# Cosine attention with a gated MLP: norms of batch 0 by Ln and Exp, pair by pair, with copies and casts on other engines

## The chip, the cores and the metric

The kernel runs on one core of a Trainium2 chip. The metric is the device time of one execution in microseconds; lower is better. A core has five engines that work side by side, each in the order of its own instructions: TensorE (PE in the profile, with its weight loads apart as PEld), VectorE (DVE), ScalarE (ACT), GpSimd (POOL) and SyncE (SP), which here only issues DMA transfers. Times inside the kernel are counted from the start of the span.

## The reference

Eight batches, twelve heads, 448 tokens, head width 64. Attention works on q and k that are divided by their own norms; its output, with the heads side by side, goes through a two-layer MLP with the gate h * sigmoid(1.702 h).

```python
q_n = q / (np.linalg.norm(q, axis=-1, keepdims=True) + 1e-06)
k_n = k / (np.linalg.norm(k, axis=-1, keepdims=True) + 1e-06)
scores = np.matmul(q_n, k_n.transpose(0, 1, 3, 2)) / tau
scores = scores - np.max(scores, axis=-1, keepdims=True)
attn = np.exp(scores)
attn = attn / (np.sum(attn, axis=-1, keepdims=True) + 1e-09)
attn_out = np.matmul(attn, v)
# x: (B*S, H*D) = (3584, 768); w_in: (768, 2048); w_out: (2048, 768)
h = x @ w_in
g = h * (1.0 / (1.0 + np.exp(-1.702 * h)))
out = g @ w_out
```

tau is 0.1. All inputs and the output are float32.

## The kernel before

The unit of attention is a pair of heads: 48 pairs, six to a batch, numbered 0 to 47. A pair is loaded as three tiles, q, k and v, each of 112 partitions x 2 heads x 4 chunks x 64 (`load`, L227, 224 KB each). Then, for q and for k:

- ACT squares the tile (`square`, L235), DVE sums each row (`reduce`, L240).
- The sums of a group of pairs go together through the norms, which are wholly on DVE: an integer estimate of the inverse root, two Newton steps, and three operations for the 1e-6 (`norm_a` L252, `newton` L268, `norm_b` L278): ten DVE operations a group, whatever its size. For batch 0 the groups are pair 0; pairs 1 and 2; pairs 3, 4 and 5 (L608). Batch 1 has groups of two, the rest groups of three.
- POOL multiplies the tile with the inverse norm to float16 (`scale`, L291). Only q of pair 0 is scaled on DVE.
- For pairs 0 to 11, PE transposes the scaled tiles against an identity (`transposes`, L310) and DVE copies the result out (`transposed`, L325). Later pairs are transposed by DMA (`dma_transposed`, L329).

v is cast to float16 into a tile that holds ones for the softmax sums (`cast_v`, L302): by ACT for batch 0, by POOL later. There are six such v tiles.

Batches 0 and 1 run attention in halves of 224 query columns: `scores_h` on PE (L386), `exp` on ACT (L352), `attend_h` on PE (L402), `normalise_h` on DVE (L417), a transposition of the result back by PE (`turn_h`, L429), and a copy of this turned half into xT (`turned_h`, L438). In batch 0 the first half's copy is ACT's, the second half's DVE's. All first halves of batch 0 come ahead of the second ones, so that the MLP of batch 0 can begin on half the tokens. From batch 2 on attention runs on whole pairs, with the softmax sums exchanged through DRAM for three pairs at a time.

The MLP is a first product (`mm1_h` L525 for batch 0, `mm1` L496 for the others), a Tanh on ACT (L507), a gate on DVE (L513, L537), a second product (`mm2`, L550), and a copy with the factor 0.5 on ACT (`halve`, L562) before the store. A product of batch 0 needs the halves of all six pairs.

The order of the instructions is made before the program runs, by `Plan` (L36): every step is added with its engine, a cost in microseconds, a due time, what it follows, and which slots of buffers it takes and frees. The planner runs through these costs and takes, on each engine, the ready step that is due first. The order that comes out is then fixed on every engine, whatever the chip does. Some of its details matter here:

- Where PE has nothing to do for over 0.3 us of the plan within its first 50 us, it puts in transposes of the identity that nobody reads, to keep PE busy (`fill`, L322, and L57).
- Loads of q, k and v are issued by SP in one fixed order (`turn=True`); only q of pair 0 is issued by ACT. The w_in matrix (3 MB in two halves, L588) and w_out (the same, L594) are issued by POOL, in POOL's own order. w_in is held until q of pair 4 has landed, w_out until q of pair 11 has (L772 to L775).
- Pairs 6 to 8 may be loaded only when the first half of w_in has landed, pairs 9 to 11 when the second has, and pair 12, and what is behind it in SP's order, when w_out has (L620).
- The resource "port" (L607) keeps steps of POOL and norms of DVE from being planned side by side: what takes it on POOL is made to wait for the last step of DVE that took it (L66).

```python
groups = [(0,), (1, 2), (3, 4, 5)]
...
hold = [("w_in", int(x >= HP + 3))] if HP <= x < 2 * HP else [("w_out", 1)] if x == 2 * HP else []
```

Of the kernel before, what the change touches and what calls it, by code (L numbers as in the profile page):

```python
# [35 lines left out]
class Plan:  # L36
# [117 lines left out]
def kernel(  # L154
# [10 lines left out]
    nc = tc.nc  # L165
# [4 lines left out]
    P = 112  # L170
    C = S // P
    HP = H // 2
# [3 lines left out]
    NQK = 7  # L176
    HALF = 2 * HP
    AHEAD = 3
    TURN = 2 * HP
    SH = S // 2  # L180
    inv_tau = float(1.0 / tau)
# [6 lines left out]
    pool = lambda name, bufs: ctx.enter_context(tc.tile_pool(name=name, bufs=bufs))  # L188
# [5 lines left out]
    p_in = pool("p_in", NQK)  # L194
    p_v = pool("p_v", 4)
    p_sq = pool("p_sq", 2)
    p_n = pool("p_n", 2)
    p_qks = pool("p_qks", 3)
    p_qkT = pool("p_qkT", 7)
    p_exp = pool("p_exp", 8)  # L200
# [24 lines left out]
    q32, k32, v32, sqs, n2s, nrms, rss, qkss, qkTs = [{} for _ in range(9)]  # L225

    def load(x, d, src, nm):  # L227
# [4 lines left out]
            in_=src[b, h0 : h0 + 2].rearrange("h (p c) d -> p h (c d)", p=P),  # L232
        )

    def square(x, ti):  # L235
        sqs[x, ti] = p_sq.tile([P, 2, C, D], FP32, name="sq")
        src = (q32, k32)[ti][x]
        return nc.scalar.activation(out=sqs[x, ti], in_=src, func=AF.Square)  # L238

    def reduce(x, ti):  # L240
# [37 lines left out]
    def norm_b(grp):  # L278
# [9 lines left out]
            rss[x] = yv[:, x - grp[0]]  # L288
        return last

    def scale(x, ti, eng):  # L291
        if x not in qkss:
            qkss[x] = p_qks.tile([P, 2, C, 2, D], FP16, name="qks")
        src = (q32, k32)[ti].pop(x)
        return eng.tensor_tensor(  # L295
            out=qkss[x][:, ti].rearrange("p c j d -> p j c d"),
            in0=src,
            in1=rss[x][:, ti, :, :, None].to_broadcast((P, 2, C, D)),
            op=ALU.mult,
        )  # L300

    def cast_v(x):  # L302
        src = v32.pop(x)
        vt = vts[x % NV]
        copy = nc.scalar.copy if x < HP else nc.gpsimd.tensor_copy
        return tuple(
            copy(out=vt[:, :, j, 64 * j : 64 * j + D], in_=src[:, j]) for j in range(2)  # L307
        )
# [129 lines left out]
    def turned_h(x, h):  # L438
        b, hp = x // HP, x % HP
        if h == 0:  # L440
            xTs[b, hp] = p_x.tile([128, S], FP16, name=f"xT{hp}")
        (nc.scalar.copy if b + h == 0 else nc.vector.tensor_copy)(
            out=xTs[b, hp][:, h * SH : (h + 1) * SH],
            in_=avps.pop((x, h))[:, 384:].bitcast(FP16)[:, :SH],
        )
# [159 lines left out]
    )  # L605
    add = plan.add
    port = dict(takes=[("port", 1)], frees=[("port", 1)])  # L607
    groups = [(0,), (1, 2), (3, 4, 5)]  # L608
    groups += [tuple(range(g, g + 2)) for g in range(HP, HALF, 2)]
    groups += [tuple(range(g, g + GRP)) for g in range(HALF, NPAIR, GRP)]  # L610
    group_of = {x: g for g in groups for x in g}
# [5 lines left out]
    for x in range(NPAIR):  # L617
        s, grp, g, first = due_of(x), group_of[x], x // GRP, x < HP
        early = due_of(grp[0]) - (4 if first else 8)
        hold = [("w_in", int(x >= HP + 3))] if HP <= x < 2 * HP else [("w_out", 1)] if x == 2 * HP else []  # L620
        for ti, nm in ((1, "k"), (0, "q")):
            add(("load", nm, x), "ACT" if x + ti == 0 else "SP", 0.5, s - 13, partial(load, x, (q32, k32)[ti], (q, k)[ti], nm + "32"),
                takes=[(nm, 1)], dma=PAIR, hold=hold, turn=True)
            add(("sq", ti, x), "ACT", 0.53, early + ti * 0.1, partial(square, x, ti),
                after=[("load", nm, x)], takes=[("sq", 1)])
            add(("red", ti, x), "DVE", 0.6, early + 0.2, partial(reduce, x, ti),
                after=[("sq", ti, x)], frees=[("sq", 1)])
            dve = x == 0 and ti == 0
            add(("scale", ti, x), "DVE" if dve else "POOL", 0.7 if dve else 1.0, early + 0.5 if first else s - 5 - ti * 0.1,
                partial(scale, x, ti, nc.vector if dve else nc.gpsimd),  # L630
                after=[("norm", 1, grp)], takes=[("qks", 1), ("port", 1)], frees=[(nm, 1), ("port", 1)])
        if x == grp[0]:
            reds = [("red", ti, y) for y in grp for ti in range(2)]
            n = len(grp)
            add(("norm", 0, grp), "DVE", 0.78 + 0.06 * n, early + 0.3, partial(norm_a, grp), after=reds, **port)
            add(("norm", 1, grp), "DVE", 1.14 + 0.18 * n, early + 0.3, partial(norm_b, grp), after=[("norm", 0, grp)], **port)
        add(("load", "v", x), "SP", 0.5, s - 9, partial(load, x, v32, v, "v32"),
            takes=[("v", 1)], dma=PAIR, hold=hold, turn=True)
        add(("cast", x), "ACT" if first else "POOL", 0.64 if first else 0.75, s - 0.5, partial(cast_v, x),
            after=[("load", "v", x)], takes=[("vt", 1), ("port", 1 - first)], frees=[("v", 1), ("port", 1 - first)])  # L640
        if x < TURN:
            add(("tp", x), "PE", 0.4, s - 3, partial(transposes, x),
                after=[("scale", 0, x), ("scale", 1, x)], takes=[("a", 1), ("qkT", 1)], frees=[("qks", 2)])
            add(("qkT", x), "DVE", 0.6, s - 3, partial(transposed, x), after=[("tp", x)], frees=[("a", 1)])
        else:
            add(("qkT", x), "SP", 1.3, s - 3, partial(dma_transposed, x),
                after=[("scale", 0, x), ("scale", 1, x)], takes=[("qkT", 1)], frees=[("qks", 2)],
                dma=packets(2 * P, C * D * 4))
        if x < HALF:
            for h in range(2):  # L650
# [12 lines left out]
                add(("turn", x, h), "PE", 0.15, sh + 1, partial(turn_h, x, h), after=[("nx", x, h)],  # L663
                    frees=[("xs", 1)])
                add(("x", x, h), "ACT" if first and not h else "DVE", 0.35, sh + 1, partial(turned_h, x, h), after=[("turn", x, h)],
                    takes=[("x", 1 - h)], frees=[("mm", 1)])
            continue
        for c in range(C):
            add(("s", x, c), "PE", 0.19, s + c // 2, partial(scores, x, c), after=[("qkT", x)],
                takes=[("sp", 1)], frees=[("qkT", int(c == C - 1))], rows=64)  # L670
# [100 lines left out]
    for i in range(2):  # L771
# [2 lines left out]
        add(("w_out", i), "POOL", 1.0, 9 + i, partial(load_w_out, i), hold=[("load", "q", 2 * HP - 1)],  # L774
            dma=packets(1024, 3072), **port)  # L775

    make_identity(nc, ident)
    for vt in vts:
        nc.vector.memset(vt[:, :, 0, D:128], 0.0)
# [46 lines left out]
```

## Time and profile before

| What | Value |
|---|---|
| Median of 8 runs | 479.57 us (475.34 to 480.99) |
| Profiled execution, its own time | 480.99 us |
| Its span | 479.1 us |
| Busy: PE, ACT, DVE, POOL | 97%, 65%, 58%, 28% of the span |
| TensorE clock granted, mean | 0.989 of full speed |
| DMA moved | 63.50 MB, 133 GB/s over the span |
| Exp of the scores (L355, ACT) | 192 x 917 ns |
| Squares (L238, ACT) | 96 x 635 ns |
| Row sums (L244, DVE) | 96 x 678 ns |
| Scaling (L295, POOL) | 95 x 1046 ns |
| Cast of v on POOL (L307) | 84 x 401 ns |
| Identity transposes (L323, PE) | 326 x 234 ns |

Successive instructions overlap in the records: matmuls and transposes are issued much closer together than their single durations, and an ACT or DVE operation starts up to some 0.1 us before the record of the one before it ends. Where a step's place in a queue counts, the distance from start to start is what matters. A share of busy time says little about PE, since the identity transposes count as busy too. In brackets behind an instruction the timelines give the idle time before it and what ended it.

### The profile page before, as it was taken

How to read it: one execution, taken by the hardware profiler on the slowest of the kernel's cores; microseconds unless marked ns; L12 is line 12 of the kernel's file. 1: busy time of each engine (PE TensorE's matmuls, PEld its weight loads, DVE VectorE, ACT ScalarE, POOL GpSimd, SP SyncE). 2: the span in 40 equal slices, each digit the busy share in tenths (PEclk: the TensorE clock that was granted, in tenths of full speed). 3: DMA queues.
4: the chain of work that ended last, by engine and by line, in shares of the span. 5: the costliest groups of instructions: out<-in, count | busy, mean ns of one | idle time of the engine just before them, and what ended most of it. 6: DMA issues, size and time to landing. Idle time of an engine off the chain costs nothing.

```text
span 479.1 us, 9003 instructions
## 1 busy us (share of the span) xinstructions
PE 463.0 (97%) x3382; PEld 267.8 (56%) x3382; DVE 276.0 (58%) x663; ACT 310.3 (65%) x491; POOL 132.2 (28%) x189
## 2 busy tenths in 40 slices
PE   8789999899999999999999999999999999999996
PEld 8767889664444554445444554445444554555563
DVE  6736986787688635875495636963373315532500
ACT  4669978789897567876778567865666556423411
POOL 1450761657624322406151422415110000000000
PEclk9999999799999999999999999999999999999999
DMA  9999597989978557446564567343310222012022
GB/s 200 227 228 251 92 207 212 256 231 206 230 148 138 142 133 187 117 103 192 145 152 109 140 158 186 96 123 97 88 44 3 62 68 63 2 62 67 1 57 76
DMA packets 81435, 63.50 MB, mean 133 GB/s; under 512 B 40232, under 2 KB 74864, under 8 KB 81392
## 3 DMA queue, kind: packets, MB, share of 16 engines
q1 hardware_dynamic: 77504, 56.41, 47.9%
q0 software_dynamic: 3648, 6.29, 7.3%
q8 instruction: 26, 0.43, 0.4%
q10 hardware_dynamic: 240, 0.23, 0.1%
q14 instruction: 17, 0.14, 0.1%
HBM read 49.81 MB, written 11.14 MB: 127 GB/s over the span
## 4 chain that ended last, share of the span: by engine, by line
PE 75%; DMA 9%; DVE 5%; ACT 4%; POOL 2%; issue 2%; SPq 2%; ACTq 0%; POOLq 0%; DVEq 0%
PE mm L554 27%; PE mm L499 23%; PE avp L363 9%; PE sp L344 6%; DMA q<-in_q_dram 3%; DMA k<-in_k_dram 3%; PE mm L529 3%; PE mm L409 3%; ACT expT L355 2%; POOL qks L295 2%; DMA v<-in_v_dram 2%; PE sp L392 2%; DVE xT L487 1%; ACT sq L238 1%; PE tps L323 1%
## 5 line engine op out<-in xcount | busy, mean ns | idle before, releaser
L355 ACT ACTIVATE expT<-sp 112x896 f16<-112x896 f32 x192 | 166.7, 917 | 57.1 <-PE sp L344 45.8
L554 PE MATMUL mm<-w_out,gT 128*128 128x384 f16 x896 | 153.8, 326 | 0.0
L499 PE MATMUL mm<-xT,w_in 128*128 128x448 f16 x672 | 134.0, 353 | 1.1 <-DVE gT L516 0.9
L554 PEld LDWEIGHTS <-gT 128*128 128x128 f16 x896 | 84.1, 98 | 65.4 <-issue 13.0
L499 PEld LDWEIGHTS <-w_in 128*128 128x128 f16 x672 | 63.1, 98 | 67.7 <-issue 12.8
L516 DVE SCALAR_TENSOR_TENSOR gT<-th,mm 128x448 f16<-128x448 f16 x112 | 67.9, 618 | 57.0 <-ACT th L509 56.5
L509 ACT ACTIVATE th<-mm 128x448 f16<-128x448 f32 x128 | 69.4, 545 | 37.8 <-PE mm L499 31.4
L244 DVE TENSOR_REDUCE n<-sq 112x8 f32<-112x512 f32 x96 | 64.2, 678 | 38.5 <-ACT sq L238 38.0
L307 POOL CAST vt<-v 112x256 f16<-112x256 f32 x84 | 32.3, 401 | 160.8 <-PE avp L363 102.0
L380 DVE TENSOR_SCALAR av<-avp 65x448 f16<-65x448 f32 x72 | 44.5, 618 | 47.7 <-PE avp L363 47.4
L363 PE MATMUL avp<-expT,vt 112*128 112x448 f16 x288 | 66.6, 352 | 0.7 <-DVE av L380 0.6
L295 POOL TENSOR_TENSOR qks<-k,y 112x512 f16<-112x512 f32 x48 | 50.2, 1045 | 57.7 <-DVE y L285 33.2
L565 ACT ACTIVATE ost<-mm 128x384 f32<-128x384 f32 x56 | 27.5, 491 | 43.7 <-PE mm L554 42.1
L295 POOL TENSOR_TENSOR qks<-q,y 112x512 f16<-112x512 f32 x47 | 49.2, 1047 | 6.6 <-DVE xT L487 6.6
L344 PE MATMUL sp<-qkT 64*112 64x448 f16 x288 | 43.0, 372 | 0.0
L363 PEld LDWEIGHTS <-vt 112*128 112x128 f16 x288 | 27.8, 97 | 25.6 <-issue 1.3
L238 ACT ACTIVATE sq<-k 112x512 f32<-112x512 f32 x48 | 30.4, 636 | 13.4 <-DMA k<-in_k_dram 10.4
L487 DVE TENSOR_TENSOR xT<-av,rcb 64x448 f16<-64x448 f16 x72 | 31.4, 437 | 10.6 <-DMA rcb<-rcp 9.6
L238 ACT ACTIVATE sq<-q 112x512 f32<-112x512 f32 x48 | 30.2, 635 | 9.5 <-DMA q<-in_q_dram 6.7
L323 PE MATMUL tps<-ident 128*128 128x128 f16 x326 | 23.5, 234 | 5.8 <-DVE qkT L327 4.3
L344 PEld LDWEIGHTS <-qkT 64*112 64x112 f16 x288 | 13.1, 124 | 27.8 <-issue 27.5
L409 PE MATMUL mm<-vt,expT 112*112 112x65 f16 x384 | 25.7, 222 | 0.5 <-ACT expT L355 0.4
(39 smaller groups left out, 231.1 us busy)
## 6 DMA issues: line engine op xcount, KB each, us to landing
k<-in_k_dram SPq DMA_DIRECT2D x48, 224.0 KB, 2.9
v<-in_v_dram SPq DMA_DIRECT2D x48, 224.0 KB, 3.3
q<-in_q_dram SPq DMA_DIRECT2D x47, 224.0 KB, 4.9
rcb<-rcp SPq DMA_DIRECT2D x24, 168.0 KB, 3.2
w_in<-in_moe_w_in_dram POOLq DMA_DIRECT2D x2, 1536.0 KB, 17.5
w_out<-in_moe_w_out_dram POOLq DMA_DIRECT2D x2, 1536.0 KB, 14.8
out_dram<-ost SPq DMA_DIRECT2D x7, 336.0 KB
out_dram<-ost SPq DMA_DIRECT2D x8, 288.0 KB
```

The costliest lines, as they stand in the source:

```text
L238: return nc.scalar.activation(out=sqs[x, ti], in_=src, func=AF.Square)
L244: nc.vector.tensor_reduce(out=n2s[grp][:, x - grp[0], ti], in_=sqs.pop((x, ti)), axis=AX.X, op=ALU.add,)
L295: return eng.tensor_tensor(out=qkss[x][:, ti].rearrange("p c j d -> p j c d"), in0=src, in1=rss[x][:, ti, :, :, None].to_broadcast((P, 2, ...
L344: nc.tensor.matmul(out=sp[:, j, :S], lhsT=qkT[64 * j : 64 * (j + 1), 1, c * P : (c + 1) * P], rhs=qkT[64 * j : 64 * (j + 1), 0, :], start= ...
L355: nc.scalar.activation(out=e, in_=sps.pop(key)[:, :, :S], func=AF.Exp, scale=inv_tau, **kw)
L363: nc.tensor.matmul(out=ps, lhsT=vts[x % NV][:, c, j], rhs=exps[x, c][:, j], start=(c == 0), stop=(c == C - 1),)
L380: nc.vector.tensor_scalar(out=avs[x][:n, j], in0=ps[:n], scalar1=AV_SCALE, scalar2=None, op0=ALU.mult)
L409: nc.tensor.matmul(out=ps[:P, o : o + D + 1], lhsT=exps[x, h, c // 2][:, j, at : at + P], rhs=vts[x % NV][:, c, j, 63 * j : 63 * j + D + 1 ...
L499: nc.tensor.matmul(out=ps[:, :S], lhsT=w_in_sb[:, kk, 128 * m : 128 * (m + 1)], rhs=xTs[b, kk], start=(kk == 0), stop=(kk == KT1 - 1),)
L509: nc.scalar.activation(out=ths[key], in_=mms[key][:, :S], func=AF.Tanh, scale=0.851)
L516: nc.vector.scalar_tensor_tensor(out=gts[b // 2][:, m, (b % 2) * S : (b % 2 + 1) * S], in0=ths.pop((b, m)), scalar=1.0, in1=mms.pop((b, m) ...
L554: nc.tensor.matmul(out=mms[b2, t, n][:, :NW], lhsT=gts[b2][:, kk, 128 * t : 128 * (t + 1)], rhs=w_out_sb[:, kk, NW * n : NW * (n + 1)], st ...
```

## The change

It has three parts, all in the head of the kernel.

1. The norms of the six pairs of batch 0 are made pair by pair. ACT takes Ln of the sums and then Exp of half of it, which is the norm (`root`); DVE adds 1e-6 and takes the reciprocal (`inverse`). These take the place of the ten DVE operations, and they do not take the "port". A table set that holds Ln and Exp is loaded by ACT as its first instruction. The pool of the small norm tiles has three buffers instead of two. Later batches keep their norms.
2. The first halves' copies into xT in batch 0 are DVE's, like the others (`XA` is empty).
3. ACT casts v of pairs 0 and 1 only (`CA`), POOL that of all others.

The switch that could put squares on POOL (`SQP`) is empty, so it does nothing. As all this goes through the planner, the order changes on every engine. In the changed order, 259 identity transposes stand on PE where there were 326; POOL issues the first half of w_in after the scaling of pair 1, where it was after that of k of pair 0; and ACT has two loads of tables, one at its start and one before the first Tanh, where it had one.

```diff
+    SQP, SQT, XA, CA = (), (0, 1), (), (0, 1)
...
-    p_n = pool("p_n", 2)
+    p_n = pool("p_n", 3)
...
+    def root(grp):
+        a = n2s[grp]
+        nc.scalar.activation(out=a, in_=a, func=AF.Ln)
+        nc.scalar.activation(out=a, in_=a, func=AF.Exp, scale=0.5)
+
+    def inverse(grp):
+        a = n2s.pop(grp)
+        y = p_n.tile([P, len(grp), 2, 2, C], FP32, name=f"yv_{len(grp)}")
+        nc.vector.tensor_scalar(out=y, in0=a, scalar1=1e-6, scalar2=None, op0=ALU.add)
+        last = nc.vector.reciprocal(out=y, in_=y)
+        for x in grp:
+            rss[x] = y[:, x - grp[0]]
+        return last
...
-        copy = nc.scalar.copy if x < HP else nc.gpsimd.tensor_copy
+        copy = nc.scalar.copy if x in CA else nc.gpsimd.tensor_copy
...
-        (nc.scalar.copy if b + h == 0 else nc.vector.tensor_copy)(
+        (nc.scalar.copy if x in XA and not h else nc.vector.tensor_copy)(
...
-    groups = [(0,), (1, 2), (3, 4, 5)]
+    groups = [(x,) for x in range(HP)]
...
+            if first:
+                add(("norm", 0, grp), "ACT", 0.48, early + 0.3, partial(root, grp), after=reds)
+                add(("norm", 1, grp), "DVE", 0.45, early + 0.3, partial(inverse, grp), after=[("norm", 0, grp)])
+        if x == grp[0] and not first:
             add(("norm", 0, grp), "DVE", 0.78 + 0.06 * n, early + 0.3, partial(norm_a, grp), after=reds, **port)
             add(("norm", 1, grp), "DVE", 1.14 + 0.18 * n, early + 0.3, partial(norm_b, grp), after=[("norm", 0, grp)], **port)
...
-        add(("cast", x), "ACT" if first else "POOL", 0.64 if first else 0.75, s - 0.5, partial(cast_v, x),
-            after=[("load", "v", x)], takes=[("vt", 1), ("port", 1 - first)], frees=[("v", 1), ("port", 1 - first)])
+        ca = x in CA
+        add(("cast", x), "ACT" if ca else "POOL", 0.64 if ca else 0.75, s - 0.5, partial(cast_v, x),
+            after=[("load", "v", x)], takes=[("vt", 1), ("port", 1 - ca)], frees=[("v", 1), ("port", 1 - ca)])
...
-                add(("x", x, h), "ACT" if first and not h else "DVE", 0.35, sh + 1, partial(turned_h, x, h), after=[("turn", x, h)],
+                add(("x", x, h), "ACT" if x in XA and not h else "DVE", 0.35, sh + 1, partial(turned_h, x, h), after=[("turn", x, h)],
...
+    nc.scalar.preload_act_table_set("natural_log_exp_and_others")
     make_identity(nc, ident)
```

More of the change, by code (lines that the diff above doesn't have):

```diff
@@ L233, in load, with sq_pool @@
         )
+    def sq_pool(x, ti):
+        return x in SQP and ti in SQT
     def square(x, ti):
@@ L237, in square @@
         src = (q32, k32)[ti][x]
+        if sq_pool(x, ti):
+            return nc.gpsimd.tensor_tensor(out=sqs[x, ti], in0=src, in1=src, op=ALU.mult)
         return nc.scalar.activation(out=sqs[x, ti], in_=src, func=AF.Square)
@@ L623 @@
                 takes=[(nm, 1)], dma=PAIR, hold=hold, turn=True)
-            add(("sq", ti, x), "ACT", 0.53, early + ti * 0.1, partial(square, x, ti),
-                after=[("load", nm, x)], takes=[("sq", 1)])
+            pl = sq_pool(x, ti)
+            add(("sq", ti, x), "POOL" if pl else "ACT", 1.0 if pl else 0.53, early + ti * 0.1, partial(square, x, ti),
+                after=[("load", nm, x)], takes=[("sq", 1), ("port", int(pl))], frees=[("port", int(pl))])
             add(("red", ti, x), "DVE", 0.6, early + 0.2, partial(reduce, x, ti),
```

## The prediction

> **What bounds the kernel now.** I read the page first: its share of busy time and the forty slices.
>
> ```profile
> PE 463.0 (97%) x3382; PEld 267.8 (56%) x3382; DVE 276.0 (58%) x663; ACT 310.3 (65%) x491; POOL 132.2 (28%) x189
> ...
> PEclk9999999799999999999999999999999999999999
> DMA  9999597989978557446564567343310222012022
> ```
>
> PE is never idle for long after the head, so time can be gained only where PE does nothing useful. But busy is not useful: 326 transposes of the identity (L323) only keep PE warm, nearly all in the first 48 us. The DMA row says that the head also fills the DMA engines. The stage windows, cut at the events found below, separate this (columns: window, length, busy us of PE, PEld, DVE, ACT, POOL, then granted clock, DMA share, GB/s):
>
> ```profile
> 20.00:44.76 24.76, 20.15 (x288) 16.67 (x284) 11.82 (x33) 17.21 (x32) 8.06 (x10) 0.93 1.12 237
> 44.76:84.70 39.94, 38.74 (x526) 34.86 (x525) 33.12 (x96) 33.22 (x52) 18.17 (x26) 1.00 0.85 179
> 84.70:94.00 9.30, 6.97 (x58) 5.73 (x58) 6.61 (x19) 6.92 (x11) 6.57 (x10) 0.64 1.21 263
> 94.00:479.00 385.00, 379.25 (x2239) 193.19 (x2238) 210.34 (x459) 241.92 (x380) 93.06 (x133) 1.00 0.45 114
> ```
>
> From 94 us on PE is full. Between 84.7 and 94 it has 6.97 us at a mean clock of 0.64, some 4.5 us of full-speed work: 4.8 us lost. The rest of the loss is the head, read in the timelines of DVE, POOL and PE:
>
> ```profile
> 22.96 0.21 DVE L274 SCALAR_TENSOR_TENSOR y<-t,y 112x48 f32<-112x48 f32 x1
> 26.05 0.62 DVE L327 COPY qkT<-tps 128x896 f16<-128x896 f16 x1 [2.88 <-PE tps L315]
> ...
> 28.46 1.04 POOL L295 TENSOR_TENSOR qks<-k,y 112x512 f16<-112x512 f32 x1 [7.18 <-DVE y L285]
> ...
> 33.46 1.04 POOL L295 TENSOR_TENSOR qks<-q,y 112x512 f16<-112x512 f32 x1
> ...
> 44.76 1.32 PE L529 MATMUL mm<-xT,w_in 128*128 128x224 f16 x12
> ```
>
> The norms of pairs 3 to 5 form one group. Its second half stands on DVE behind a copy that waits 2.88 us for PE; POOL idles 7.18 us and delivers the last scaled pair only at 34.5 (33.46+1.04). The first MoE product starts at 44.76. Last, the waits of SP's queue:
>
> ```profile
> SPq L230 <- DMA w_in<-in_moe_w_in_dram: 13.4, 2, 10.7
> ```
>
> Batch 1 may load only when w_in has landed. In the DMA view the two halves are issued at 14.13 and 16.40 and take 14.3 and 20.8 us; the first q of batch 1, issued at 28.80, takes 8.9 us, to 37.7. At some 0.95 us a load, k of pair 6 lands at about 36.8. DMA moves 230 GB/s here: no faster norm moves this.
>
> **What the skill says.** "ScalarE: Activation LUTs", Table sets: Ln and Exp share natural_log_exp_and_others, Tanh with Exp is in exp_and_others. So two loads are to be expected, not one; the changed instruction order shows exactly two, at the start and before the first Tanh. Its section on ACT_TABLE_LOAD gives 1283 ns, and 1.28 us is what the trace shows; its further 1.38 us of drain no row of the trace shows, and I leave it in the range. "TensorE: Matmul & The Clock Gate", What's actually happening: after about 3.4 us of idleness PE runs at half clock. The trace agrees in kind: clock 0.64 after the stall at 84.7. "Perfetto Trace Analysis", Tensor Engine Instruction: ACT, DVE and GpSimd are strict FIFO. The trace agrees (the DVE copy above holds the norm behind it), and my sum hangs on this.
>
> **The change, part by part.** The sum is against the profiled execution: 480.99 us (span 479.1 and 1.9 around it), 1.4 above the median of 479.57.
>
> *Norms.* Batch 0 loses 3 x 10 DVE operations, 2.1 to 2.4 us of chain each (6.56 to 8.69 for the first), 6.9 us in all. It gains 6 x 2 on DVE: add 0.17 and reciprocal 0.25, 0.45 with the gap between them (8.03 to 8.48 before), 2.7 us; and 6 x 2 on ACT. No 112x16 ACTIVATE is in the trace: the section's 186 ns + 0.833 ns per element makes an estimate of 0.2 us each, 2.4 in all; its other bound is the 0.32 us of the 128x224 copy, 3.8 in all. I take 0.2.
>
> *Copies and casts.* Six xT copies leave ACT (6 x 0.23 from start to start: 1.4 us) for DVE (6 x 0.27), which is idle there half the time. Four pairs' casts leave ACT (8 x 0.30: 2.4 us) for POOL (4 x 0.74 from its own rows), ahead of the fifth pair's scales. ACT gains 3.8 and pays 2.4 + 1.28: about even. The cover for the POOL casts is its idle time; gone, 3.0 us would fall on the last pair. The free end is POOL contention with DVE, which these rows already contain.
>
> *Where that leads, walked with these durations.* The preload now stands ahead of q0's DMA on ACT's queue: 0 to 1.3 us later. PE hides it: 127 fills in place of 145, at 70 ns (10.16/145), end at 10.3, before 11.5. POOL then goes without gaps: w_in's first half at 14.1 (it waits for the q load of pair 4 as before), 1.0; scales of pair 2 to 17.0; second half 0.8; pairs 3 and 4 to 21.9; two casts 1.5; pair 5 to 25.3, not 34.5. ACT reaches its third exp at 19.2 and runs 10 exps (0.81 each), a square and a root (0.9) to 28.2. Attend, normalise, turn and copy of pair 5 (0.81+0.6+0.26+0.27, with hand-overs) put the first product at 31, 13.8 us earlier.
>
> *What takes it back.* In the new order ACT holds, after 15 exps and no Tanh, the square of k of pair 6, which lands at 36.8. ACT gets there at about 31 and stands; behind it are exp 16, the table load and the first Tanh, so PE stops after two products (33.6). From 36.8 to exp 24 ACT has 9 exps (7.3), 8 squares (4.2), 4 Tanh (1.7) and the load (1.3): 14.5 us, to 51.3. The tenth and eleventh attends need exp 22, 3.1 us sooner (48.2); they take 1.6, the transposes of pair 6 0.5 (its scales: square of q7 at 44.2, reduce 0.6, ten norm operations 2.4, two scales 2.0: 49.5), and some half-clock work about 1. The fifth product starts at 51.5; before it starts at 56.77, with the same eleven attends but one transposed pair more (0.5). Lead: 4.8 us.
>
> *Further on.* POOL issues w_out after pair 7's scales (51.5) and two casts (1.5): 53.0, before 54.06. So batch 2's loads gain only 1.1 us, and its first square, at 77.69 before, can start at 76.6 or a little sooner. The order puts that square two exps and a Tanh later than before (2.0): ACT asks at 77.69-4.8+2.0 = 74.9. Before, its load had been issued at 73.20 and took 2.7, to 75.9; 74.8 now. The lead just fits. Then the 4.8 us lost at 84.7 to 94: there PE stood with twelve score matmuls ordered ahead of the next attend; the new order has eight, and puts attends sooner. Nothing back at all, or all 4.8: I take 1.6. From 94 on PE is full in the same order, and keeps the lead.
>
> Sum: 4.8 + 1.6 = 6.4. 480.99 - 6.4 = 474.6 for the profiled time; 479.57 - 6.4 = 473.2 for the median. **Forecast: 473.2.**
>
> **Rivals.** *The lead is hidden by DMA*: w_out and batch 2's loads bind, so only the 1.1 us of the w_out issue remain: 478.5. For it: DMA share 1.1 in the head and 1.21 at 84.7; against: that first pair of batch 2 is used only at 103.7 (L344), and PE has products to fill with.
>
> *More*: PE keeps most of the 13.8 and none is lost at 84.7, if k of pair 6 lands early: 13.8 - 5.7 (its wait, the overlap with other work given back) + 4.8 is 12.9 at most; with half of the last, 469. Against: the DMA bound above.
>
> *Slower*: the squares hold ACT twice. If w_out is issued after about 55.5, because the half clock and the stall at k of pair 6 delay pair 7's scales, batch 2's squares, standing ahead of exps in ACT's queue, hold PE at 75 us: an idle of about 4 us and a half-clock stretch of 6.8 us (87.3 to 94.1 before) costing 3.4, on top of the present loss and less the 4.8 lead: +2.6, and with the drain 1.4, 483.6. It decides from the point where the wait exceeds the lead.
>
> *It doesn't do what it says*: tables would switch at every Exp after Tanh, 1.28 us each. The order has two loads; I count it in the slower case.
>
> **Numbers.** Forecast 0.58 (own range 470 to 477); more 0.12; hidden 0.17; slower 0.13. Under 0.5% (2.4 us, about what can be told from no change) is the hidden case: faster 0.70, same 0.17, slower 0.13. The range 468 to 480.5 leaves out the slower case and the far end of "more".
>
> **What would show it.** Last pair scaled near 25 us; first product near 31; a gap on ACT ending at the square of k6 near 37, with half clock; table load about 1 us later; fifth product near 51.5; w_out at 53; less loss around 80 to 90. A first product after 38, or w_out after 55.5, makes me wrong.

## The result and the profile after

The changed kernel takes 473.59 us, the median of 11 runs (471.03 to 474.91). The kernel before took 479.49 us beside it (475.32 to 481.47, 32 runs). The ratio is 0.988 with a 95% interval of 0.9855 to 0.9905: faster by 1.2%, or 5.9 us in the medians. The forecast was 473.2. The profiled execution of the changed kernel took 475.07 us (span 473.2), that of the kernel before 480.99 (span 479.1), so the two traces differ by the same 5.9 us. Executions of one kernel differ by over 1%, along with their mean granted clock (the kernel before, beside the last experiments: from 475.38 us at 0.999 to 481.57 at 0.988), and both profiles are of executions some 1.5 us above their medians, at 0.989 and 0.996.

Beside the experiments below the kernel before took 478.49, 478.21 and 478.00 us (medians of 41, 17 and 42 runs). The ratios given are those on record, of runs taken together; they are not exactly quotients of two medians.

From the page of the changed kernel, the busy line, the granted clock and the DMA row:

```profile
PE 457.5 (97%) x3315; PEld 261.6 (55%) x3315; DVE 274.4 (58%) x651; ACT 308.5 (65%) x490; POOL 135.0 (29%) x197
...
PEclk9998999999999999999999999999999999999999
...
DMA  9999498999973766456653765443301212022022
```

Shares of busy time hardly moved. PE's busy time fell by 5.5 us, of which 4.5 are identity transposes that are no longer there (259 with 19.0 us, before 326 with 23.5). The clock row had a 7 in its eighth slice (84 to 96 us); now it has an 8 in the fourth (35 to 47 us). The stage windows show where (columns as in the prediction; the first window ends at the first MLP product in both kernels):

```profile
20.00:33.92 13.92, 13.48 (x205) 10.85 (x203) 8.39 (x26) 9.76 (x15) 6.83 (x12) 1.00 1.12 222
33.92:84.70 50.78, 47.41 (x616) 41.34 (x615) 38.20 (x107) 40.38 (x62) 19.70 (x30) 0.97 0.91 200
84.70:94.00 9.30, 9.30 (x117) 6.72 (x118) 8.72 (x28) 8.82 (x14) 6.42 (x8) 1.00 1.15 236
94.00:473.10 379.10, 370.68 (x2137) 186.99 (x2133) 205.22 (x444) 235.92 (x374) 92.30 (x133) 1.00 0.46 115
```

The stretch before the first product is 10.8 us shorter. The stretch from there to 84.7 is 10.8 us longer (50.78 against 39.94). From 84.7 to 94, PE is now busy all 9.30 us at full clock, where it had 6.97 us at 0.64. The last stretch is 5.9 us shorter, which only says that the span is, but PE has 8.4 us without work in it (379.10 - 370.68), where it had 5.75. Four lines from the timelines of DVE, POOL and PE show the head itself:

```profile
23.71 0.22 DVE L306 TENSOR_SCALAR yv<-n 112x16 f32<-112x16 f32 x1
...
25.45 1.04 POOL L316 TENSOR_TENSOR qks<-q,yv 112x512 f16<-112x512 f32 x1
...
53.21 1.82 POOL L617 DMA_DIRECT2D w_out<-in_moe_w_out_dram  x2
...
33.92 1.31 PE L550 MATMUL mm<-xT,w_in 128*128 128x224 f16 x12
```

The last pair of batch 0 is scaled at 26.5 us, before at 34.5. The head start shrinks and grows again on the way; these starts on PE tell how:

| Event on PE | Before | After | Lead | Lead forecast |
|---|---|---|---|---|
| First product (L529, now L550) | 44.76 | 33.92 | 10.8 | 13.8 |
| Fifth product | 56.77 | 52.40 | 4.4 | 4.8 |
| 13th product | 78.3 | 74.2 | 4.1 | |
| 16th product | 90.01 | 81.19 | 8.8 | |
| First scores of batch 2 (L344, now L365) | 103.68 | 96.24 | 7.4 | 6.4 |
| First whole product of batch 1 (now L520) | 125.49 | 117.84 | 7.7 | 6.4 |
| End of the span | 479.1 | 473.2 | 5.9 | 6.4 |

The column "before" is of one execution, and its head was at half clock from 22.4 to 25.9 us. The order-only run further below has the same order on every engine up to the first product, and on PE up to the 15th; its trace is at full clock there. The same 16 identity transposes in the kernel before, and in that run:

```profile
22.40 1.86 PE L323 MATMUL tps<-ident 128*128 128x128 f16 x16 [2.00 <-DVE qkT L327]
```

```profile
21.25 1.05 PE L323 MATMUL tps<-ident 128*128 128x128 f16 x16 [1.47 <-DVE qkT L327]
```

The order-only run has the first, the fifth and the 13th product at 42.06, 54.08 and 75.60, each 2.7 us sooner than the kernel before. So 2.7 us of the first three leads belong to this execution of the kernel before and not to the change: against a head at full clock they are 8.1, 1.7 and 1.4 (and 7.6, 2.6 and 2.3 for a second profile of the changed kernel, which has no half clock either).

Three questions follow. Is it the short norms that start the head earlier? What takes 6.4 us back between the first and the fifth product? And what gives 4.7 us between the 13th and the 16th?

### The profile page after: what moved, and what is told of

It reads as the page before. It is cut to its first block, busy times and chain, and to the rows that moved or that the text cites. A ratio compares the mean times of both kernels' runs of the same rounds, so it can differ in the third digit from the quotient of the medians.

```text
span 473.2 us, 8860 instructions
## 1 busy us (share of the span) xinstructions
PE 457.5 (97%) x3315; PEld 261.6 (55%) x3315; DVE 274.4 (58%) x651; ACT 308.5 (65%) x490; POOL 135.0 (29%) x197
## 4 chain that ended last, share of the span: by engine, by line
PE 82%; DVE 7%; DMA 4%; ACT 3%; issue 2%; SPq 1%; POOL 0%; POOLq 0%; ACTq 0%; DVEq 0%
PE mm L575 29%; PE mm L520 23%; PE avp L384 9%; PE sp L365 6%; PE mm L550 4%; PE mm L430 4%; DMA q<-in_q_dram 4%; PE tps L344 3%; PE sp L413 2%; DVE n L250 2%; ACT expT L376 1%; ACT sq L244 1%; DMA k<-in_k_dram 1%; PE tps L336 1%; DVE gT L537 1%
## 5 line engine op out<-in xcount | busy, mean ns | idle before, releaser
L376 ACT ACTIVATE expT<-sp 112x896 f16<-112x896 f32 x192 | 166.8, 916 | 51.0 <-PE sp L365 42.8
L520 PE MATMUL mm<-xT,w_in 128*128 128x448 f16 x672 | 134.3, 353 | 3.1 <-DVE gT L537 3.1
L520 PEld LDWEIGHTS <-w_in 128*128 128x128 f16 x672 | 63.1, 98 | 70.0 <-issue 15.3
L250 DVE TENSOR_REDUCE n<-sq 112x8 f32<-112x512 f32 x96 | 63.7, 678 | 34.6 <-ACT sq L244 34.0
L328 POOL CAST vt<-v 112x256 f16<-112x256 f32 x92 | 35.1, 401 | 157.1 <-PE avp L384 96.6
L401 DVE TENSOR_SCALAR av<-avp 65x448 f16<-65x448 f32 x72 | 44.4, 617 | 50.2 <-PE avp L384 49.9
L316 POOL TENSOR_TENSOR qks<-k,y 112x512 f16<-112x512 f32 x42 | 43.9, 1046 | 48.3 <-DVE y L291 34.3
L316 POOL TENSOR_TENSOR qks<-q,y 112x512 f16<-112x512 f32 x42 | 44.0, 1047 | 5.1 <-DVE xT L508 5.1
L365 PE MATMUL sp<-qkT 64*112 64x448 f16 x288 | 43.2, 372 | 1.3 <-ACT expT L376 1.3
L244 ACT ACTIVATE sq<-k 112x512 f32<-112x512 f32 x48 | 30.4, 635 | 15.6 <-DMA k<-in_k_dram 15.5
L365 PEld LDWEIGHTS <-qkT 64*112 64x112 f16 x288 | 13.3, 124 | 28.9 <-issue 28.1
L430 PE MATMUL mm<-vt,expT 112*112 112x65 f16 x384 | 24.0, 218 | 0.1
L430 PEld LDWEIGHTS <-expT 112*112 112x112 f16 x384 | 22.7, 133 | 1.3 <-issue 0.9
```

The source lines that it names most:

```text
L250: nc.vector.tensor_reduce(out=n2s[grp][:, x - grp[0], ti], in_=sqs.pop((x, ti)), axis=AX.X, op=ALU.add,)
L316: return eng.tensor_tensor(out=qkss[x][:, ti].rearrange("p c j d -> p j c d"), in0=src, in1=rss[x][:, ti, :, :, None].to_broadcast((P, 2, ...
L365: nc.tensor.matmul(out=sp[:, j, :S], lhsT=qkT[64 * j : 64 * (j + 1), 1, c * P : (c + 1) * P], rhs=qkT[64 * j : 64 * (j + 1), 0, :], start= ...
L376: nc.scalar.activation(out=e, in_=sps.pop(key)[:, :, :S], func=AF.Exp, scale=inv_tau, **kw)
L401: nc.vector.tensor_scalar(out=avs[x][:n, j], in0=ps[:n], scalar1=AV_SCALE, scalar2=None, op0=ALU.mult)
L430: nc.tensor.matmul(out=ps[:P, o : o + D + 1], lhsT=exps[x, h, c // 2][:, j, at : at + P], rhs=vts[x % NV][:, c, j, 63 * j : 63 * j + D + 1 ...
```

## Experiments: which part of the change does it

**The norms pair by pair, but on DVE as before.** From the changed kernel; no Ln, no Exp of the norms, no preload:

```diff
-    p_n = pool("p_n", 3)
+    p_n = pool("p_n", 6)
...
-            if first:
-                add(("norm", 0, grp), "ACT", 0.48, early + 0.3, partial(root, grp), after=reds)
-                add(("norm", 1, grp), "DVE", 0.45, early + 0.3, partial(inverse, grp), after=[("norm", 0, grp)])
-        if x == grp[0] and not first:
+        if x == grp[0]:
...
-    nc.scalar.preload_act_table_set("natural_log_exp_and_others")
```

> The changed kernel, but the norms of batch 0 stay the ten DVE operations, now once for each pair (60 operations instead of 30), with no Ln, no Exp of the norms and one table load. It parts 'pair by pair' from 'on ACT'. Theory A (the gain needs the short DVE chain): 60 operations of 0.21 us are 12.6 us of DVE in the head, the last pair is scaled at about 33 us or later and the first product stands near 44 or later: 479 to 484 us. Rival (small groups alone free the last pair): the first product before 38 and 474 to 476.

Measured: 483.85 us, ratio 1.0126 (1.0097 to 1.0155): slower than the kernel before, at the slow end of theory A. The last pair of batch 0 is scaled at 38.1 us (before 34.5), the first product starts at 50.0, the fifth at 61.3. Its group line for the identity transposes (busy us, mean ns, idle before them):

```profile
L344 PE MATMUL tps<-ident 128*128 128x128 f16 x443 | 29.8, 230 | 4.9 <-DVE qkT L348 3.5
```

There are 443 of them where the kernel before had 326: that many more gaps of PE had to be filled. Pair by pair without the short chain is a loss: six chains of ten DVE instructions stand in DVE's queue in place of three. It is the two-instruction chain that makes the small groups pay.

**The norms alone, and the moves alone.** The first gives ACT its copies and casts back; the second keeps the moved copies and casts, with the norms and groups of before:

```diff
 norms alone
-    SQP, SQT, XA, CA = (), (0, 1), (), (0, 1)
+    SQP, SQT, XA, CA = (), (0, 1), tuple(range(HP)), tuple(range(HP))
 moves alone
-    groups = [(x,) for x in range(HP)]
+    groups = [(0,), (1, 2), (3, 4, 5)]
...
-            if first:
-                add(("norm", 0, grp), "ACT", 0.48, early + 0.3, partial(root, grp), after=reds)
-                add(("norm", 1, grp), "DVE", 0.45, early + 0.3, partial(inverse, grp), after=[("norm", 0, grp)])
-        if x == grp[0] and not first:
+        if x == grp[0]:
...
-    nc.scalar.preload_act_table_set("natural_log_exp_and_others")
```

> The changed kernel with the copies of the first halves and all casts of batch 0 put back on ACT: the norms alone. Theory A (the norms bring the gain, the moves are about even on ACT): first product at 34 to 36 us, 473 to 475.5. Rival (the moves relieve ACT by 3.8 us and bring half the gain): 476 to 478.

> The kernel before with the other two parts of the change alone: first-half copies on DVE, casts of pairs 2 to 5 on POOL; norms as before. Theory A: the last pair is still scaled at 34 to 36 us, the first product stays at 43 to 46, the loss at 84 to 94 stays since the order from the seventh product on is that of the kernel before: 478.5 to 480.5. Rival (the moves count): 475.5 to 477.5.

Measured: norms alone 475.13, ratio 0.9956 (0.9931 to 0.9982), first product 36.5, fifth 52.6, 16th 81.6. Moves alone 476.56, ratio 0.9972 (0.9939 to 1.0004), first product 42.8, 16th 87.6, with half clock from 84.7 to 91.6, where the kernel before has it from 87.3 to 94.1. The norms carry most of the earlier head: 8.3 of 10.8 us against the trace of the kernel before, 5.6 of 8.1 against the same head at full clock (42.06). With them alone the 16th product has its lead already. On top of the norms the moves take the first product 2.6 us further (36.5 to 33.9), of which 0.2 are left at the fifth; alone they do not bring it forward (42.8 against 42.06). Alone, their gain in time can't be told from none, though it is rather 1.3 us (0.28%) than the nothing that theory A gave them.

## Experiments: the loss at 84 to 94 us

In the kernel before, PE waits in this place for exps that stand in ACT's queue behind squares of batch 2, and then runs at half clock. From its PE timeline:

```profile
86.33 0.40 PE L392 MATMUL sp<-qkT 64*112 64x224 f16 x4 [1.65 <-ACT expT L355]
...
88.50 1.71 PE L409 MATMUL mm<-vt,expT 112*112 112x65 f16 x16
...
90.01 2.43 PE L529 MATMUL mm<-xT,w_in 128*128 128x224 f16 x12
```

1.71 us for an attend and 2.43 for a product are nearly double the 0.98 and 1.31 us that the same rows take elsewhere. Between the 15th product and the next attend its order has five groups of four score matmuls, the changed order two. (The prediction set twelve matmuls against eight; its twelve are the last three groups alone, so it is twenty against eight.) So the kernel before was given one edit that changes nothing but the order, the squares of batch 2 due 2 us later:

```diff
-        early = due_of(grp[0]) - (4 if first else 8)
+        early = due_of(grp[0]) - (4 if first else 6 if 2 * HP <= x < 3 * HP else 8)
```

> The kernel before with one due time changed: the squares, sums and norms of batch 2 are planned two units later. All of the change's parts are absent. On PE the order is that of the kernel before up to the fifteenth product; then the attend of pair 9's first half stands ahead of three groups of scores and not behind them, as in the changed kernel. Theory B (the loss at 84 to 94 us came from that order: scores wait for exps, and the attend and product that could run wait behind them): that loss shrinks by 2 to 4 us, its half-clock stretch with it, 475.5 to 477.5 us though the head is as slow as before. Rival (the loss came from the late head and batch 2's data, and only a faster head removes it): no change, 478.5 to 480.

Measured: 476.22, ratio 0.9945 (0.9917 to 0.9973), with the first product at 42.1 and the 16th at 83.8. From its PE timeline:

```profile
86.50 0.40 PE L392 MATMUL sp<-qkT 64*112 64x224 f16 x4 [0.92 <-ACT expT L355]
86.83 1.02 PE L409 MATMUL mm<-vt,expT 112*112 112x65 f16 x16
```

The wait is 0.92 where it was 1.65 with two more behind it, the attend takes 1.02, and no half clock is left after 80 us. One trace could have missed it by luck, but of the 14 runs ten have a mean clock of 0.998 or more, of the 17 of the kernel before beside them three. This supports theory B: the loss was a matter of the order, and about 2.6 us of time were to be had without any new norm. The changed kernel got them as a by-product, since its plan comes out in another order.

That leaves the question whether moves and order would have been enough. This kernel has both, with the norms of before (the edits of "moves alone", and the line above):

> The kernel before with its norms and groups, but with the moved copies and casts (476.6 alone) and with the squares of batch 2 due two microseconds later (476.2 alone). Theory A (the changed kernel's gain is the sum of an order in which the loss at 84 to 94 us goes, and of an earlier head; the norms are needed for the second only): no half clock after 80 us, first product at 42 to 43, 474 to 476. Theory B (copies, casts and order are enough, the norms were not needed): 473 to 474, as the changed kernel.

Measured: 475.57, ratio 0.995 (0.9932 to 0.9968), first product 43.1, 16th 85.0, no half clock after 80 us. Theory A holds: this is no better than the order alone (0.9945), and its interval lies above that of the changed kernel (0.9855 to 0.9905). The norms are needed for the rest.

## Experiments: what takes the head's lead back

The forecast named a stand of ACT at the square of k of pair 6. From ACT's timeline of the changed kernel, and below it PE's:

```profile
33.68 0.92 ACT L376 ACTIVATE expT<-sp 112x896 f16<-112x896 f32 x1 [1.60 <-PE sp L413]
35.31 0.63 ACT L244 ACTIVATE sq<-k 112x512 f32<-112x512 f32 x1 [0.71 <-DMA k<-in_k_dram]
...
36.76 1.28 ACT L530 ACT_TABLE_LOAD   x1
38.06 0.54 ACT L530 ACTIVATE th<-mm 128x448 f16<-128x448 f32 x1
...
49.69 0.94 ACT L376 ACTIVATE expT<-sp 112x896 f16<-112x896 f32 x1
```

```profile
39.46 0.60 PE L413 MATMUL sp<-qkT 64*112 64x224 f16 x4 [1.42 <-ACT expT L376]
39.99 2.42 PE L550 MATMUL mm<-xT,w_in 128*128 128x224 f16 x12
```

ACT stood 0.71 us for that load, not 5.8. Then came the second table load, and PE stood 1.42 us for an exp and ran at half clock from 39.5 to 42.9. Three kernels vary that load. The first takes it away: Ln is replaced by Exp in the norms of batch 0, so these norms are other numbers, and one table set serves all.

```diff
-        nc.scalar.activation(out=a, in_=a, func=AF.Ln)
+        nc.scalar.activation(out=a, in_=a, func=AF.Exp)
...
-    nc.scalar.preload_act_table_set("natural_log_exp_and_others")
+    nc.scalar.preload_act_table_set("exp_and_others")
```

> The changed kernel with Exp in place of Ln in the norms of batch 0, so that one table set serves all and the second load is gone; the norms of batch 0 are then wrong numbers, the work and the order are the same. It prices the second load with all that hangs on it. Theory A: 1.3 us of ACT at 36.8, 1.4 us of PE idle and up to 1.7 us of half clock: 470.5 to 472.5. Rival (ACT waits there anyway): 473 to 474.

The second keeps Ln and puts the load behind the 14th exp, where ACT waited 1.60 us for PE anyway:

```diff
 in exp(), after the activation
+        if len(exps) == 13:
+            nc.scalar.preload_act_table_set("exp_and_others")
```

> The changed kernel with the second table load put after the fourteenth exp of the scores, where ACT stood idle for 1.60 us at 32.1 to 33.7 waiting for PE; the order is otherwise the same on every engine. Theory A (the load costs only where ACT has work queued): the load is hidden, the stall of PE at 38 to 39.5 us and the half-clock stretch after it go, 471.5 to 473 us, mean clock near 1. Rival (in whatever place, the load brings PE under the activity that keeps its clock up): as with the load at 23 us, 476 to 479.

The changed kernel itself ran beside them once more:

> The changed kernel itself, beside the others on the same chip. Theory A and its rivals all expect 472 to 474.5 us and a mean clock of 0.996 to 1.0; it shows how far one chip's times can be held against another's.

Measured: one table 471.69 (470.92 to 471.99), ratio 0.9827 (0.9767 to 0.9887); load in the gap 471.46 (471.15 to 471.80), ratio 0.9827 (0.9778 to 0.9877); the changed kernel 473.74 (471.45 to 474.32), ratio 0.9866 (0.9811 to 0.9921). Fifth product at 49.9, 49.3 and 51.5. From ACT's timeline of the load in the gap:

```profile
31.48 1.28 ACT L380 ACT_TABLE_LOAD   x1
33.06 0.92 ACT L376 ACTIVATE expT<-sp 112x896 f16<-112x896 f32 x1 [0.30 <-PE sp L415]
```

ACT still waits 0.30 us for PE after the load: it is hidden whole. In its place before the first Tanh it costs about 2 us by the medians (473.74 - 471.69 and 473.74 - 471.46), more than its own 1.28; these are medians of four runs each, and the intervals of the ratios overlap. At the fifth product the lateness needs no half clock: in this second profile of the changed kernel, PE waits 0.68 us at 39.19 and 0.58 at 41.43, no half clock follows, and the fifth product is late all the same. But that profiled execution took 471.45 us, as little as the versions without the load in that place, though its 16th product is still late (80.27, against 78.08 with the load in the gap). So a late fifth product need not cost time at the end, and where the 2 us of the medians are lost stays open. The version with the load in the gap is faster than the kernel before and, by its median, than the changed one.

The third puts the load earlier still, right behind the last norm of batch 0:

```diff
-        nc.scalar.activation(out=a, in_=a, func=AF.Exp, scale=0.5)
+        last = nc.scalar.activation(out=a, in_=a, func=AF.Exp, scale=0.5)
+        if grp == (HP - 1,):
+            nc.scalar.preload_act_table_set("exp_and_others")
+        return last
```

> The changed kernel with the second table load (the set with Exp and Tanh) put right after the last root of batch 0, at about 23 us on ACT, in place of right before the first Tanh at 36.8; the order is otherwise the same on every engine. Theory A (the load at 36.8 holds exps back and with them PE, 1.4 us idle and a half-clock stretch that costs 1.7): the stall is smaller and the fifth product 1 to 3 us sooner; 471 to 473. Rival (ACT waits for k of pair 6 and for PE anyway, and at 23 us the load delays the exps of pairs 3 to 5 by the same 1.3 us): no change, 473 to 474.

Measured: 478.73 (472.05 to 482.07, 21 runs), ratio 0.9981 (0.9948 to 1.0014). Both theories missed: the whole gain is gone. From the stage windows, and from the timelines of ACT and PE:

```profile
26.00:43.40 17.40, 17.15 (x150) 13.82 (x150) 4.95 (x16) 8.79 (x12) 2.86 (x7) 0.51 1.12 249
```

```profile
23.87 1.28 ACT L303 ACT_TABLE_LOAD   x1
...
26.14 0.43 PE L416 MATMUL sp<-qkT 64*112 64x224 f16 x4 [1.23 <-ACT expT L379]
...
27.11 1.67 PE L433 MATMUL mm<-vt,expT 112*112 112x65 f16 x16
```

Here ACT had no gap. The load put off three exps, PE stood 1.23 us, and then ran at half clock for 17.1 us although it was busy 17.15 of 17.40 us. The first product slid to 40.3. It is this half clock that costs: 20 of the 21 runs have a mean clock of 0.975 to 0.982, and the one with 0.998 took 472.05 us. The load costs nothing or some 7 us (478.73 against 471.69 without it), by where it stands and whether PE's clock is halved behind it.

**Is ACT what bounds 34 to 48 us?** In the version with the load in the gap ACT is busy 13.71 of these 14 us. Two kernels take squares of batch 1 off ACT and put them on POOL, of pairs 6 to 8 and of pairs 6 and 7:

```diff
 load in the gap, and
-    SQP, SQT, XA, CA = (), (0, 1), (), (0, 1)
+    SQP, SQT, XA, CA = (6, 7, 8), (0, 1), (), (0, 1)
```

> The version with the table load in the gap (471.5), and the squares of q and k of pairs 6 to 8 on GpSimd instead of ScalarE. Theory A (ScalarE bounds from 34 to 48 us, in a row without gaps there: six squares of 0.63 less is up to 3.8 us): fifth product at 46 to 48 instead of 49.3, and 469 to 470.5 in time, if the rest of the lead is kept. Theory B (ScalarE is full, but the keys of batch 1, and with them the queue of w_out, then come later by GpSimd's slower squares, so that what is won in the head is lost at the first pairs of batches 1 and 2): 471.5 to 475.

> As the run with the squares of pairs 6 to 8 on GpSimd, but of pairs 6 and 7 alone. Theory A: between that run and 471.5, in proportion: four squares of 0.63 are 2.5 us, 470 to 471. Theory B (GpSimd's slower squares put off w_out): less late than with three pairs, 471 to 473.

Measured: three pairs 474.38, ratio 0.9925 (0.9893 to 0.9958); two pairs 470.93, ratio 0.9839 (0.9793 to 0.9884), not to be told from the 0.9827 without them. With three, the fifth product starts at 46.4, as theory A had it, and the time is theory B's. Its timelines of DVE and PE show where the lead goes:

```profile
58.51 0.19 DVE L291 TENSOR_TENSOR y<-y,t 112x32 f32<-112x32 f32 x1
...
60.90 0.62 DVE L564 SCALAR_TENSOR_TENSOR gT<-th,mm 128x448 f16<-128x448 f16 x1
...
61.56 1.29 PE L432 MATMUL mm<-vt,expT 112*112 112x65 f16 x16 [1.44 <-DVE gT L564]
```

Two norm chains of batch 1 now stand back to back on DVE, from 56.35 to 60.98, and a gate behind them; PE waits for the gate, runs at half clock from 62.0 for 3.4 us, and the 16th product is at 81.1 where it was at 78.1. So it was not w_out alone (issued at 52.82 instead of 50.46) as theory B said, but the ten-instruction chain again; what the later w_out adds was not tried. With two pairs, the fifth product came at 50.6 and not earlier: ACT had fewer squares but waited for scores (0.97 us at 37.52). A full ACT in this stretch is then no proof that ACT alone sets its length; the two engines hand on to each other, and the order decides.

**The identity transposes.** The version with the load in the gap, without any of them:

```diff
-WARM_FROM, KEEP_WARM, FILL_US, FILL_SPARE = 1.5, 50.0, 0.056, 0.3
+WARM_FROM, KEEP_WARM, FILL_US, FILL_SPARE = 1.5, 0.0, 0.056, 0.3
```

> The version with the table load in the gap (471.5), without any of the transposes of the identity that nobody reads; the other work is the same and in the same order, and the outputs too. Theory A (they keep the clock up: without them TensorE starts its first products at half clock): half clock through most of the first 40 us, fifth product 1 to 3 us later, 473 to 478. Theory B (in the head TensorE waits for others anyway, so that a half clock there costs nothing): 471 to 472.5.

Measured: 477.35, ratio 0.9978 (0.9957 to 0.9998), against 0.9827 with them. First product 38.0 instead of 33.3, fifth 55.0 instead of 49.3. Theory A, though the fifth product lost more than it allowed: PE ran at half clock once more from 50.7 to 57.5 us, where the other version has 44 identity transposes between 42 and 50 us, and that product took 2.45 us. A window and a line from its trace, then the same from the version with them:

```profile
20.00:34.00 14.00, 13.67 (x124) 10.85 (x124) 5.79 (x18) 7.70 (x12) 6.14 (x12) 1.00 1.12 231
...
25.75 1.71 PE L432 MATMUL mm<-vt,expT 112*112 112x65 f16 x16
```

```profile
20.00:34.00 14.00, 13.58 (x205) 11.23 (x204) 7.66 (x24) 11.02 (x14) 6.34 (x12) 1.00 1.12 227
...
24.68 0.98 PE L432 MATMUL mm<-vt,expT 112*112 112x65 f16 x16
```

PE is as busy in both, and the clock column says 1.00 in both. But an attend takes 1.71 us without them and 0.98 with them, so PE gets through 124 instructions instead of 205. Without the identity transposes PE is slow up to about 40 us; the trace's first entry of the clock is only at 40.45 us (4.17 with them), and the column shows 1.00 where there is no entry. That they count as busy work and yet are useful is what the busy share could not tell.

## Why the prediction was right, point by point

**Norms: right.** The small Ln and Exp of 112x16 take 0.20 to 0.22 us each (0.2 taken). Add and reciprocal take 0.22 and 0.25 for the last pair (0.17 and 0.25 taken); the add took 0.33 and 0.77 for pairs 3 and 4, the cause of which is not shown. The last scaling starts at 25.45 (25.3 was forecast for its end, so the end is 1.2 us late).

**The preload: right that it costs nothing.** It stands ahead of q's load on ACT's queue but did not hold it back: the load's issue is at 0.77, the table load runs from 0.74 to 2.02, and the first square of q starts at 5.07 (5.12 before).

**Copies and casts: "about even" holds at the fifth product, not for the whole.** There, norms alone stand at 52.6 and all three parts at 52.4. But the times are 0.9956 and 0.988 of the kernel before, and the intervals do not meet. By the ratios some 0.8% of the time comes with the moves, then, more than the moves alone gained (0.28%); by the medians, 475.13 and 473.59, it is 1.5 us (0.3%). The profiles do not show where: norms alone have their first scores of batch 2 at 95.0, all parts at 96.24, and at 95.33 in their second profile. This stays open.

**The first product, 31: mis-sized, 33.9.** The walk let ACT run its exps without a wait. It waited for PE's scores 0.73, 1.27 and 0.53 us before the twelfth exp, the last that the first product needs, which ended at about 30.4 (28.2 forecast).

**The stand at k of pair 6: failed in size.** The step "ACT gets there at about 31 and stands" gave 5.8 us; measured 0.71. ACT came there at 34.6, for the waits above and one more of 1.60 us, and the load landed at 35.3 where 36.8 was forecast. So the stretch that the step counts from there began 1.5 us early.

**From there to the fifth product: right in kind, the end by luck.** From the square of k of pair 6 to the end of exp 24 it was 15.2 us (35.31 to 50.49, where the next square starts), 14.5 forecast, with the same nine exps, eight squares, four Tanh and one load, and a wait of 0.55. The half clock was there (3.4 us, some 1.7 of work lost, about 1 forecast). The fifth product came at 52.40 (51.5 forecast), so from the square to it were 17.1 us and not 14.7; part of the rest is a wait of PE for a DVE copy, 0.79 us at 52.29. The late end and the early start nearly cancel. The lead was 4.4 against 4.8, but that 4.8 was counted against the 56.77 of one trace, whose half clock at 22.4 the prediction did not price; 2.7 us of the lead are that. w_out was issued at 53.21 (53.0).

**Batch 2's first square: not as forecast, without harm.** It ran at 77.61, not 74.9, because ACT was waiting for PE's scores and products there (0.71 us ahead of the exp before it). "The lead just fits" was not put to the test; the lead was 4.1 us at the 13th product either way.

**The loss at 84.7 to 94: the term mis-sized.** "Nothing back at all, or all 4.8: I take 1.6" gave a middle between two cases. The lead rose from 4.1 at the 13th product to 7.4 at the first scores of batch 2: 3.3 came back. The reason given, the order of scores and attends, is what the order-only run confirms.

**"From 94 on PE ... keeps the lead": failed by 1.5 in this execution.** The lead of 7.4 ended as 5.9. PE had new waits, the largest of which are these:

```profile
107.39 0.40 PE L365 MATMUL sp<-qkT 64*112 64x448 f16 x2 [1.28 <-ACT expT L376]
...
183.96 2.24 PE L520 MATMUL mm<-xT,w_in 128*128 128x448 f16 x11 [1.47 <-DVE gT L537]
```

The second was 0.45 us before. In the second profile of the changed kernel the two are 0.68 and 0.78 us, and a lead of 8.4 at the first scores of batch 2 ended as 9.5, so this loss is not in every execution. In the two traces compared the sum came out right, 5.9 for 6.4, by two terms that missed in opposite directions: 1.7 more at 84 to 94 than taken, 1.5 less afterwards; 0.4 less at the fifth product and 0.3 lost from there to the 13th make the rest. Of the rivals, "more" was right on k of pair 6 landing early and on the loss at 84.7 going, and wrong that PE keeps most of the 13.8. "Hidden by DMA" was right that batch 2 hardly gains (w_out issued 0.85 us sooner, its first square at 77.61 for 77.69), and wrong that no more than this is left: PE kept a lead over that stretch. "Slower" had its half clock, but w_out was issued well ahead of its 55.5. The tables were loaded twice, not at every Exp.

About half of the 5.9 us is clock. The mean granted clock over the span was 0.989 before and 0.996 after in the two profiles: 479.1 x 0.011 = 5.3 against 473.2 x 0.004 = 1.9, so an estimated 3.4 us less time lost to it. The rest, 2.5 us, is fewer waits. The runs say much the same: at a mean clock of 0.998 or more the kernel before takes 476.46, 476.62 and 476.47 us (medians of 11 such of 41, 3 of 17 and 8 of 42 runs, beside the three sets of experiments), the changed one 473.5 (10 such of its first 12). So some 3 us of the gain are there at full clock too; the other 3 come because the changed kernel loses the clock less often. The prediction's 6.4 is close to the whole, but it put at most 1.6 us of it to the clock.

## What to carry to other kernels

A chain of many short instructions in a queue of strict order costs most by what it puts off behind it: shorten the chain first, and only then make the groups small. In the warm-up of a kernel an earlier start is worth what is left of it at the next shared bound, so follow the lead event by event and do not add it up at the start, and against more than one execution of the kernel before. A table load is an instruction to be placed: put it where its engine waits anyway, and look there for gaps in the trace, since a fixed cost of 1.28 us was worth from 0 to about 7 us by its place.

## What the runs showed of the hardware that was not expected

- Half clock comes in pieces of 3.4 us (3.4, 6.8 and, after the early table load, 17.1) and can follow gaps of PE of 1.2 to 2.0 us. "TensorE: Matmul & The Clock Gate", What's actually happening, has an activity window of about that length; its idle window of some 3.4 us is more than what was needed here. In every trace the changes of the clock lie whole multiples of 3.41 us apart (in the kernel before, full clock for 17.07, half for 3.41, full for 61.44, half for 6.83), and this grid starts at another time in each execution: the first entry is at 4.05 to 7.41 us in the kernels with identity transposes. In the step of the grid just ahead of each half clock during the work, PE was busy for 1.26 to 2.39 of the 3.41 us (1.42 and 1.36 in the kernel before, 2.00 in the changed one, 1.26 with three pairs' squares on POOL, 2.39 with the norms pair by pair on DVE).
- That can explain why one order is hit in one execution and not in another. The wait that ended at 22.40 in the kernel before, 2.00 us, ended at 21.25 in the order-only run with 1.47 us; there the step of the grid, 17.70 to 21.11, still had 2.08 us of work, and no half clock followed. It is no sharp limit: other steps with 1.8 to 2.4 us of work passed without half clock, in other mixtures of instructions.
- PE can stay at half clock while it is busy nearly all the time: 17.15 of 17.40 us. There the stretch ended about 3 us after the first MLP product had started (40.3 to 43.4), and 2.4 us after it in the run without the identity transposes (38.05 to 40.45). That short attends and scores do not count as enough work is only a guess; it was not tried.
- In the run without the identity transposes the clock column stays at 1.00 through a head in which PE's rows are up to 1.87 times as long (a first product of 2.45 us against 1.31). The column alone does not tell a cold PE; the duration of a known instruction does.
- A table load on ACT does not hold back the DMA issue that stands behind it (0.77 within 0.74 to 2.02). The further drain that "ScalarE: Activation LUTs", What ACT_TABLE_LOAD costs, adds to the load shows in no run: the next activation starts 0.02 us after it (38.06 after 36.76 + 1.28, and 25.17 after 23.87 + 1.28 in the early load).
